# Seven quarter products for piece 10's second layer, and a second engine for some low words

## The chip, the cores and the metric

One core of a Trainium2 chip runs the kernel. The metric is the device time of one execution in microseconds, here the median of three runs. TensorE (PE) multiplies matrices into PSUM; VectorE (DVE), ScalarE (ACT) and GpSimd (POOL) do the element work; GpSimd is given no PSUM operand in this kernel. Each engine takes its instructions in the order in which they were written for it, and a semaphore holds an instruction whose operands or buffers aren't ready.

## The reference

Block-causal attention over q, k, v of 8 batches x 8 heads x 576 x 64, and then a feed-forward network on the 4608 x 512 result:

```
scores = q k^T / sqrt(64);  blocks of 64 columns above the diagonal block are masked
x      = softmax(scores) v                         # (4608, 512), heads side by side
h      = x @ w_in                                  # first layer, 512 -> 2048
g      = h * clip(h + 3, 0, 6) / 6
out    = g @ w_out                                 # second layer, 2048 -> 512
```

Inputs and output are 32-bit floats (the weights arrive as 64-bit words). To reach that accuracy with 16-bit multiplies, the kernel splits each operand into a high word and a low word of 16 bits and adds three products, high x high, high x low and low x high.

## The kernel before

**Tiles and pieces.** The 4608 rows are 13 pieces of up to 384 rows. A piece's first layer makes h in 16 groups f of 128 hidden columns, its second layer adds g of all 16 groups into PSUM banks. Attention runs ahead of the pieces by (batch, head pair) and is done when piece 10 begins. Pieces 10, 11 and 12 (`STR`) run last.

**Plain second layer** (`ffn2_`). For each f and each of three tiles of 128 rows, six matmuls of 512 columns (three word pairs, two halves of 64 stationary columns): 48 groups of six for a piece. Before it, for each f, ACT takes the relu, DVE the product, ACT or DVE the high word and DVE the low word. At the end three banks are copied out.

**Seven quarter products.** Cut into quarters, a product of two matrices of 2 x 2 blocks can be had from seven block products instead of eight, if sums and differences of the blocks are formed first. The first layer of pieces 10 to 12 does this in `h_pair` (seven products for each pair c of groups f; a product is 12 matmuls of 192 columns; ACT and DVE bring it out of PSUM into `hf`, and DVE adds). The weights' sums are made by `w_comb` (one for each of 8 c), the rows' by `x_comb`. The second layer of pieces in `SO` does it in `o_pair`: for a pair c of groups f it runs seven products, each in a part of 256 columns (six matmuls) and a part of 128 columns (six matmuls), into six banks. `g_pair` makes its left operands: relu and product on a pair of groups at once, four sums and differences of 192 columns (`pm`, on DVE or GpSimd), and high and low words of three tiles. `t_comb` makes the combined weights of w_out, `t_homes` says where in SBUF they lie. At the end two scalings and 14 scaled additions bring the seven products into the output rows.

**The order.** The program is first recorded as a list of steps, each with one or more ways (which engine can do it). A table written out in the file, `ORDER`, says for every step in which place and on which engine it is emitted; `SLOTS` says which buffer a tile takes. So the order on each queue, and the choice of engine, are fixed by the tables. PSUM: `h_pair` takes its banks from a pool of two (`ps_h`) and one of three (`ps_s`), but from `ps_h` alone in pieces of `SO` (in the first of them from c = 2 on), since `o_pair` holds the three of `ps_s`.

**Low words of P.** In attention each row block of probabilities is written as high and low words (`phl`) and transposed by a DMA. A row block with an odd number of 64-column blocks ends in a half block of 128 x 64, whose low word is one DVE instruction (line 1156).

Of the kernel before, what the change touches and what calls it, by code (L numbers as in the profile page):

```python
# [56 lines left out]
SO = (11, 12)  # L57
# [26 lines left out]
    "%oBEx1`Qsn7?7C2QU(rmb#{wa(XnjzbcUrzT;r*er^gjO>DzDe<KQeIZ(hbzX;8A2yi_)9{Df@dip-{vi4ny`lSCzA375kcj2L-1"
    "yt!snN?zoU(PL&NrRuKaF3K+m3SOL+6Qv*97CmL<{#h}x#|*RU8>cF+wzMv3Dk~2?6BZJ>blLj$Yj9z%AFrrXTZeUYEmv!%byjWI"
    "xUaXmc4GJQIdwe^FQ(5RpW0Msd*Y<#*YC-v56pd7f8of{M}I!S#ku(S$-zUD{@yS%zZC!F^1P>*&u_ZppS_yDdyn?(%eSjn^{h!q"
    "tf^gVadVvw*0O=Q?e&ijtgTx%Z~tcXJ*oMpQpI-POQE&2PPx_g&Vyrzx4!$)v%lBy0WJjMxbc18Pw(SaI$_Yv+jj;J={NM=Fr2qG"
    "ynT6xD}BbS`?@nLR!+;!Ti_2xFv<qTC2)OL`S=Cs4J4}l&fY7DNduEp@^@V=C`_KWJ2Gm%vGYj!)Yxka7aYsHe)M>GT2WTTNKxgO"
    "(WAx|Z@jd5OE#~nx@6Pkh#_B7_w3F1CXBgoaRh($n(Ys|POe>dVr%qc!M^XaML$lZ9yoY<$DFx`4*&f1`_Hzaw}dxtzFGM8_WBKf"
    "@8sMZzxeLGclRGWd=#+=!^*aQe?4cyB))(vUXnW?udhp=e*Gia_5lN3-Ja~%m^p}-axVEsNou5${DMMj*|3RE-Q_%6bEfJ@R&^+j"  # L90
    "estM0ONR0j!OrTr4W2mI&yz&H@!{C#j~*MNhkH{TMmv7-qFxCIeDQM7V4v8Ac`>j2gI;f{RV)}Y_QVK_;E*t<ku>McqvF;#rZnqU"
    "zJm{It6?TKE#0YU@~zu-Tc%9Cvm?V#tJ_*s_UiK5%q#Pc-(5GZ{N968r_Y>SAO5i7@}tU@KlN1`+8#eS_t$LaQ+07xfAjko-1%MY"
    "nR_idW?6J%ySgt~O_<m-X)@OG!o}X{HYaVLS<g8-W%typv-eo`wd=PJPw=#|rta^5;2_bfWYA!m@1ZzK{ITOF7Lu}aj6R2t40-+L"
    "{m|UJ`~hV}@OgRruEf!`blTVQLhp6X??0R>CNKJ!;5lsjfP%z<=~UVbdj~<%C!Ec<#h=FwO3V29Wv+CCOs;?rS+a7Qi=&e^C3VK~"
    "nX`tkaO*=~Y&*MDwXyEo`0u|M9zT9Asa!Z^s!*h3vcwYhN%yKbt15oYU2s19`^X=^uNk?U7V-3(x7cm|{ow$9HPH|e8P(Y29}pcg"
    "YE1o~(Vg=y1kS&RiTyjGVVT+bHEWxzYxqI6!3Phm+e#+1w6=GUb{{@{hO>0T@)gs1yZX`1{X@F%_N?5v$$3Rzx4^UK>i6_%XbcJt"
    "33UmhY<cp`W$%uA_tpCzJb(D8&2_7`<f&%t^sMY{+u1vtLSKcubEUkOIs@m$>s@c&dJWm11Dn&#c&vWc`SH`|FGbs!{P!9TOJKZu"
    "?RsoW>y4YYZb$SHerQ{=bm*`?#ZjV;uyyTgzbaLcF(Zb{6y7_<@&ZZW`o7U4eSGh|_1oRA|DD%ed-Qia#+B~fu`6}d=mA%*j^Ta$"
    "R9=xbwz8_aW?$U2jP%;1p6+GiCk&iEqjzRqa{S#x6AxcnzH-%@UkQ_D-JhHCdG?$y*RJosG4JN%C%+HOU-0zVYWedQixkR*i&f@p"
    "^70Gl%s(Eiqi~CT^eikIeC%NH*9UHYzh^#+fh+v-)$t=IPO^1+Lt^R0(?epvG0vWQWrlI3((E11{P<}x?9*ps#Q96FFSu{__L(?o"  # L100
    "^A^Hn?87f!gT9Wm@Y{-s9BLV6Yxk|DcEkinr}`BQCC*VRt)d@Qk0X-($Dg`vz3R<({BYlZx2v1i;A{dbr)&uMxpq#~#^ZHALWA~A"
    "B{lvkOW*$|_^(<!ro5tU(^%~7mX14?cUvj^_5%l-es^|t&z(Oq-D;kuXThPvPe#QbOPKjOF81Di!2`3hY14a!BC$j&8-3#G!o;NH"
    "MT?!5I4@mx(xs2*X|F+p*R2m<xZFI0o2pPgw#FSf`fgy~eyM4Tmt+rlcm|iXblI$&Yl}|3e{??c?DE-*m)I>`Ve`T5+=YvmY%s5E"
    "EiPa8yLki4<qaj+roCw=Ua|DQnv&}(;}b@-3TCvm%Y_R9w{0g6!&_~zhCk9$kvQ5e03Sl4^e6A8NrFR(qr69tSvL0S9?}3hBb>=%"
    "zm2o^4Z4-&k+Sz%{5!Qnn5M5bf*LdYeZK)1?BprBg2J(}MaAwuoMcs5$+$@!+fO^LSk=(E!!TjuhiSd%^rho>cI{d@ef63VmE}_t"
    "Dk2lFU#wbmv%2O|ZR5%rO*2<rKC^Jmjqd(E7B_G09yV+C$L8~O0^yuJb1$5|a<x7qbHVD(+=GYiUO&8d?bfX99A55?dGq(Fm3eEA"
    "jEvG~Z{0q+<yg2_)N=36fm0IQ1HBY(>y5;Rk0wohy#M4-BR@(e|N3IG;bru;{Iqn1%Ja$4r^h{FzJ0Iw5j$egv*(+x4WDw~{O8~k"
    "8N=>)W&YZ1=JLCIxc5zp)h#M*Q`ShIvdYn8va7tUhuHVwtRMAY;B8koU%I=4W88ub3v2)U_3^FWTIc5<uq8erw7RCD$;o*m<55fF"
# [1832 lines left out]
```

## Time and profile before

| | |
|---|---|
| three runs | 952.05, 952.43 and 954.31 us, median 952.43 us |
| the profiled execution | 951.95 us, of which the span from first to last instruction is 950.2 us |
| PE busy | 942.8 us (99% of the span) |
| DVE busy | 860.0 us (91%) |
| ACT busy | 722.0 us (76%) |
| POOL busy | 98.3 us (10%) |
| granted TensorE clock | 0.999 of full |

A busy time is the union of an engine's instructions. Matmuls are pipelined and their ends are modelled, so a row's length says less than the distance from its start to the next row's start. Times are counted from the span's start. Almost every instruction stands under line 423, where the recorded steps are emitted, so rows are told apart by the tiles' names: `m` are products of `h_pair`, `hf` what they become, `o` the second layer, `rs`, `gr`, `gs` the operands that `g_pair` makes, `wr`, `wq`, `ws` the tiles of `w_comb`, `tr`, `tw` those of `t_comb` (its results go to `tq`, `tp`, `win`, `vnat`).

### The profile page before, as it was taken

What the parts mean: (1) busy time and instruction counts of PE and PEld (TensorE: products, weight loads), DVE (VectorE), ACT (ScalarE), POOL (GpSimd) and SP (SyncE); (2) the same over time, 40 slices, a digit from 0 to 9 for tenths busy, and PEclk for the clock granted to TensorE, in tenths of its full rate; (3) what the DMA queues carried; (4) which work ended last, traced back from release to release, by engine and by line L of the source; (5) the groups of instructions that cost most, each with busy time, mean ns of one, the idle gap of its engine ahead of it and who ended that gap; (6) DMA issues with size and microseconds to landing.
All of it is one profiled execution on the core that took longest, in us unless ns stands there. A gap on an engine that the chain in (4) does not pass through costs nothing.

```text
span 950.2 us, 34711 instructions
## 1 busy us (share of the span) xinstructions
PE 942.8 (99%) x14108; PEld 686.3 (72%) x14108; DVE 860.0 (91%) x2526; ACT 722.0 (76%) x1791; POOL 98.3 (10%) x283
## 2 busy tenths in 40 slices
PE   9999999999999999999999999999999999999998
PEld 7777777766677766666667666666666667789998
DVE  5988999999999999999999999999899998999987
ACT  6989898888988878888788878778665356676662
POOL 1443101100000000110000010100000102000000
PEclk9999999999999999999999999999999999999999
DMA  7877699989999999999999899986785000000001
GB/s 211 280 246 213 125 178 169 180 166 181 167 189 168 179 188 162 183 189 181 165 201 181 169 165 180 179 162 121 127 128 106 2 2 36 2 35 4 14 26 36
DMA packets 390704, 132.93 MB, mean 140 GB/s; under 512 B 373264, under 2 KB 376592, under 8 KB 390544
## 3 DMA queue, kind: packets, MB, share of 16 engines
q1 hardware_dynamic: 389456, 129.87, 71.7%
q8 instruction: 110, 1.80, 0.8%
q10 hardware_dynamic: 1088, 0.85, 0.3%
q14 instruction: 50, 0.41, 0.1%
HBM read 45.09 MB, written 9.44 MB: 57 GB/s over the span
## 4 chain that ended last, share of the span: by engine, by line
PE 97%; DMA 1%; DVE 1%; ACT 0%; issue 0%; SPq 0%; DVEq 0%
PE o L423 37%; PE h L423 30%; PE m L423 9%; PE s L423 7%; PE pv L423 6%; PE pf L423 1%; PE sf L423 1%; PE pt L423 1%; DMA qkT<-qks 1%; PE pr L423 1%; PE gm L423 0%; DMA qf<-in_q_dram 0%; PE warm L423 0%; PE o_1b L423 0%; PE o_2b L423 0%; PE o_0b L423 0%
## 5 line engine op out<-in xcount | busy, mean ns | idle before, releaser
L423 PE MATMUL o<-wout,g 128*64 128x512 f16 (+2 forms) x2760 | 346.5, 378 | 0.0
L423 PE MATMUL h<-x,win 128*64 128x384 f16 (+2 forms) x3568 | 330.1, 318 | 0.0
L423 PEld LDWEIGHTS <-win 128*64 128x64 f16 (+1 forms) x4432 | 231.7, 110 | 81.3 <-issue 1.7
L423 PEld LDWEIGHTS <-g 128*64 128x64 f16 x2784 | 154.0, 110 | 98.6
L423 DVE SCALAR_TENSOR_TENSOR phl<-p,st,phl 128x64 f16<-128x64 f32 (+4 forms) x364 | 154.9, 447 | 4.2 <-ACT phl L423 2.3
L423 ACT ACTIVATE p<-p,st 128x192 f32<-128x192 f32 (+8 forms) x252 | 139.1, 553 | 22.7 <-DVE st L423 20.7
L423 DVE CUSTOM_DVE_ANT_0 p<-s,none,esc 128x64 f32<-128x64 f32 (+7 forms) x252 | 119.9, 486 | 14.6 <-PE s L423 11.2
L423 ACT ACTIVATE r<-h,eg,sh 128x384 f32<-128x384 f32 (+1 forms) x176 | 101.5, 591 | 40.2 <-PE h L423 33.9
L423 ACT ACTIVATE phl<-p,st 128x512 f16<-128x512 f32 (+5 forms) x173 | 97.2, 582 | 11.2 <-DVE st L423 6.1
L423 PE MATMUL s<-qkT 128*64 128x512 f16 (+7 forms) x1120 | 98.5, 287 | 0.8 <-DMA qkT<-qks 0.8
L423 DVE SCALAR_TENSOR_TENSOR g<-r,g 128x384 f16<-128x384 f32 (+1 forms) x160 | 86.2, 546 | 3.8 <-ACT g L423 3.0
L423 DVE SCALAR_TENSOR_TENSOR r<-r,eg,h 128x384 f32<-128x384 f32 (+1 forms) x144 | 84.2, 586 | 5.8 <-ACT r L423 4.5
L423 ACT ACTIVATE g<-r 128x384 f16<-128x384 f32 (+1 forms) x117 | 58.3, 503 | 18.2 <-PE o L423 11.3
L423 PEld LDWEIGHTS <-qkT 128*64 128x64 f16 x1120 | 53.4, 110 | 25.1 <-DMA qkT<-qks 1.0
L423 PEld LDWEIGHTS <-vhl 128*64 128x64 f16 x1344 | 58.4, 110 | 13.4
L423 PE MATMUL pv<-pT,vhl 128*64 128x192 f16 (+2 forms) x1344 | 67.2, 233 | 0.0
L423 ACT ACTIVATE hf<-m 128x192 f32<-128x192 f32 x90 | 28.5, 327 | 36.9 <-PE m L423 31.9
L423 PEld LDWEIGHTS <-ws 128*64 128x64 f16 x1152 | 52.0, 110 | 4.1
L423 ACT ACTIVATION_READ_ACCUMULATOR p<-p,st 128x1 f32 x252 | 47.7, 189 | 0.0
L423 DVE SCALAR_TENSOR_TENSOR qks<-qk,rs_q,qks 128x576 f16<-128x576 f32 x56 | 46.8, 838 | 0.9 <-ACT qks L423 0.6
L423 PE MATMUL m<-x,ws 128*64 128x192 f16 x864 | 46.8, 246 | 0.0
L423 PE MATMUL m<-x,win 128*64 128x192 f16 x768 | 41.4, 246 | 0.4 <-DVE hf L423 0.4
(229 smaller groups left out, 1414.1 us busy)
## 6 DMA issues: line engine op xcount, KB each, us to landing
vx<-vhl SPq DMA_DIRECT2D x56, 160.0 KB, 3.4
vnat<-in_v_dram SPq DMA_DIRECT2D x63, 128.0 KB, 3.5
qk<-in_k_dram SPq DMA_DIRECT2D x28, 288.0 KB, 4.4
qk<-in_q_dram SPq DMA_DIRECT2D x28, 288.0 KB, 3.9
out_dram<-osb SPq DMA_DIRECT2D x29, 256.0 KB, 2.8
rawo<-in_moe_w_out_dram SPq DMA_DIRECT2D x13, 512.0 KB, 4.9
x<-in_moe_w_in_dram SPq DMA_DIRECT2D x9, 512.0 KB, 5.5
rawi<-in_moe_w_in_dram SPq DMA_DIRECT2D x6, 512.0 KB, 4.8
```

The costliest lines, as they stand in the source:

```text
L423: getattr(eng, method)(*args, **kw)
```

## The change

`SO` becomes (10, 11, 12): piece 10's second layer too is done by `g_pair` and `o_pair`. So `t_comb` is called before piece 10, behind `x_comb` and `w_comb`, and a part of its results gets a home in the tails of the `ws` tiles (`more`). The subtractions of `w_comb`, `x_comb` and `t_comb`, before DVE's alone in the first two, may be GpSimd's too (`plus`, `minus`). `w_comb` makes its sums in two tiles of half the size. A half block's low word may be two instructions of GpSimd: multiply in place, then subtract. In the diff below, `w_comb` and `t_homes` stand in this order; `x_comb`'s four `tensor_sub` become `minus` and `ffn_step`'s call of `t_comb` moves as said, which is left out. The tables are new: the program has 6741 steps instead of 6612, of which GpSimd has 495 instead of 277, DVE 2005 instead of 2190, ACT 1407 instead of 1380.

Read step by step, the new table gives GpSimd 95 of the 140 low words of half blocks, and of the steps recorded from piece 10's `x_comb` on 146 instead of 10 (each an addition or subtraction of two SBUF tiles): 28 `wq`, 30 `tw`, 20 `xt`, 67 `pm`, 1 `xr`. In both tables the steps of DVE and GpSimd can be counted that stand between two places: where PE has done as much work as by 690 us and as by 840 us in the trace of before (each PE step at its length there):

| step | before: DVE, GpSimd | new: DVE, GpSimd |
|---|---|---|
| `wq`, 256 columns | 32, 0 | 4, 28 |
| `tw`, 256 columns | 11, 2 | 2, 30 |
| `xt`, 192 columns | 24, 0 | 3, 20 |
| `pm`, 192 columns | 4, 0 | 0, 36 |
| `tr`, 512 columns | 7, 1 | 16, 0 |
| low words of `t_comb` | 7 | 22 |
| `wr`, of 1024 (new: 512) columns | 6, 2 | 15, 0 |
| `xr`, low words of `x_comb` | 9, 3 and 11 | 11, 1 and 10 |
| plain piece 10: product, low word | 16, 16 | none |
| `g_pair`: product, low words | 2, 1 | 10, 25 |
| attention: low words, softmax | 24, 14 | 11 (5 on GpSimd), 7 |
| high words and copies | 21 | none |

From the later place to the end: `tw` 19 before and none, `tr` 8 and none, low words of `t_comb` 11 and none, `pm` on DVE 58 and 29, on GpSimd 2 and 31, closing additions 28 and 42, high words and copies 7 and 24.

```diff
-SO = (11, 12)
+SO = (10, 11, 12)
...
             if half:
-                nc.vector.scalar_tensor_tensor(
-                    ph[:, last, BLK:], pr[:, nk - BLK:nk], r, ph[:, last, :BLK], op0=ALU.mult, op1=ALU.subtract
-                )
+                ph_, pl, pw_ = ph[:, last, :BLK], ph[:, last, BLK:], pr[:, nk - BLK:nk]
+                nc.add([
+                    ("vector", "scalar_tensor_tensor", (pl, pw_, r, ph_), dict(op0=ALU.mult, op1=ALU.subtract)),
+                    ("gpsimd", [
+                        ("tensor_scalar", (pw_, pw_, r, 1.0), dict(op0=ALU.mult, op1=ALU.mult)),
+                        ("tensor_tensor", (pl, pw_, ph_), dict(op=ALU.subtract)),
+                    ]),
+                ])
...
+    def minus(out, a, b):
+        nc.add([(e, "tensor_tensor", (out, a, b), dict(op=ALU.subtract)) for e in ("vector", "gpsimd")])
...
-        r = attp.tile([P, NDT, NH], F32, tag="qks", bufs=1, name=f"wr{c}")
-        plus(r, win[:, c, :, 0], win[:, c, :, 1])
+        wr = [ffp.tile([P, 2, NH], F32, tag="stage", bufs=NST_B, name=f"wr{c}_{j}") for j in range(2)]
+        for j, r in enumerate(wr):
+            plus(r, win[:, c, 2 * j:2 * j + 2, 0], win[:, c, 2 * j:2 * j + 2, 1])
...
-        nc.vector.tensor_add(o[:, 0], a21, a22)
-        nc.vector.tensor_sub(o[:, 1], o[:, 0], a11)
-        nc.vector.tensor_sub(o[:, 2], a11, a21)
-        nc.vector.tensor_sub(o[:, 3], a12, o[:, 1])
+        plus(o[:, 0], a21, a22)
+        minus(o[:, 1], o[:, 0], a11)
+        minus(o[:, 2], a11, a21)
+        minus(o[:, 3], a12, o[:, 1])
...
-        t = pool.tile([P, 4, 2, 2, P], F16, tag=tag, bufs=bufs, name=f"ws{c}")
+        nu = 2 if tag in ("qkT", "pT2") else 1 if tag == "pT01" else 0
+        t = pool.tile([P, 8 * 2 * P + nu * 2 * DM // 2], F16, tag=tag, bufs=bufs, name=f"ws{c}")
+        more[c] = t[:, 8 * 2 * P:].rearrange("p (i l n) -> p i l n", i=nu, l=2) if nu else None
...
-        rest += [[va[:, i]] for i in range(4)]
+        rest += [[more[3], more[5]], [more[4], va[:, :1]], [more[6], va[:, 1:2]], [more[7], va[:, 2:]]]
```

## Rows read from the trace of the kernel before

**Rows 1.** The page, part 1: busy time, share, instructions.
```profile
PE 942.8 (99%) x14108; PEld 686.3 (72%) x14108; DVE 860.0 (91%) x2526; ACT 722.0 (76%) x1791; POOL 98.3 (10%) x283
```

**Rows 2.** PE's waits, whole span: total us, times, longest us.
```profile
PE s L423 <- DMA qkT<-qks: 0.8, 1, 0.8
...
PE m L423 <- DVE hf L423: 0.4, 1, 0.4
```

**Rows 3.** Windows: length, each engine's busy us (instructions), clock, DMA.
```profile
690.00:740.00 50.00, 50.00 (x664) 32.69 (x660) 46.24 (x123) 29.61 (x68) 3.20 (x9) 1.00 0.62 106
740.00:840.00 100.00, 100.00 (x1552) 72.61 (x1548) 90.76 (x193) 56.03 (x115) 9.16 (x6) 1.00 0.03 10
840.00:945.00 105.00, 104.65 (x2481) 103.06 (x2479) 97.19 (x237) 60.56 (x131) 1.31 (x2) 1.00 0.07 21
```

**Rows 4.** PE's timeline, plain second layer: start us, modelled length us, tile, count.
```profile
815.34 3.40 PE L423 MATMUL o<-wout,g 128*64 128x512 f16 x30
818.58 0.33 PE L423 MATMUL m<-x,win 128*64 128x192 f16 x4
```

**Rows 5.** PE's timeline, seven products, parts of 256 columns.
```profile
923.37 0.52 PE L423 MATMUL o<-win,gs 128*64 128x256 f16 x6
...
924.35 1.18 PE L423 MATMUL m<-x,ws 128*64 128x192 f16 x24
```

**Rows 6.** PE's timeline, seven products, parts of 128 columns.
```profile
943.28 0.53 PE L423 MATMUL o<-win,gs 128*64 128x128 f16 x12
...
943.79 0.86 PE L423 MATMUL o<-vnat,gr 128*64 128x128 f16 x24
```

**Rows 7.** DVE's timeline, as Rows 4, in brackets idle time before.
```profile
744.71 2.37 DVE L423 SCALAR_TENSOR_TENSOR g<-r,g 128x384 f16<-128x384 f32 x1
...
787.23 2.29 DVE L423 TENSOR_TENSOR ws<-wq,ws 128x1024 f16<-128x1024 f32 x1 [0.51 <-ACT ws L423]
...
799.79 0.84 DVE L423 TENSOR_TENSOR tw<-tr,tw 128x256 f32<-128x256 f32 x1
...
912.08 0.89 DVE L423 TENSOR_TENSOR hf<-m,hf 128x192 f32<-128x192 f32 x3 [0.61 <-PE m L423]
```

**Rows 8.** POOL's timeline at the same times.
```profile
744.49 2.18 POOL L423 TENSOR_TENSOR wr<-win 128x1024 f32<-128x1024 f16 x1 [13.52 <-DVE wq L423]
...
786.13 2.31 POOL L423 TENSOR_TENSOR wr<-win 128x1024 f32<-128x1024 f16 x1 [38.28 <-DVE wq L423]
...
798.32 0.73 POOL L423 TENSOR_TENSOR tw<-tr,tr 128x256 f32<-128x256 f32 x1
...
911.99 0.60 POOL L423 TENSOR_TENSOR rs<-rs,hf 128x192 f32<-128x192 f32 x1
```

**Rows 9.** DVE's groups by shape, 690 to 945 us: count | busy us, mean ns.
```profile
L423 DVE SCALAR_TENSOR_TENSOR gs<-rs,gs 128x384 f16<-128x384 f32 x32 | 17.6, 552 | 0.1
L423 DVE SCALAR_TENSOR_TENSOR hf<-rs,eg,hf 128x768 f32<-128x768 f32 x16 | 16.2, 1015 | 0.4 <-ACT rs L423 0.4
L423 DVE SCALAR_TENSOR_TENSOR gr<-hf,gr 128x576 f16<-128x576 f32 x16 | 12.0, 752 | 0.0
...
L423 DVE TENSOR_TENSOR rs<-hf 128x192 f32<-128x192 f32 x31 | 10.5, 353 | 0.2
...
L423 DVE SCALAR_TENSOR_TENSOR r<-r,eg,hf 128x384 f32<-128x384 f32 x16 | 9.7, 614 | 0.5 <-ACT r L423 0.4
...
L423 DVE TENSOR_TENSOR wq<-wr 128x256 f32<-128x256 f32 x16 | 6.6, 419 | 0.1
L423 DVE SCALAR_TENSOR_TENSOR osb<-o,so,osb 128x256 f32<-128x256 f32 x14 | 6.5, 478 | 0.3
```

**Rows 10.** DVE's groups by shape, 0 to 740 us: the half blocks' low words.
```profile
L423 DVE SCALAR_TENSOR_TENSOR phl<-p,st,phl 128x64 f16<-128x64 f32 x140 | 39.2, 284 | 2.4 <-ACT phl L423 1.4
```

**Rows 11.** POOL's groups by shape, whole span: the nearest to the new pair.
```profile
L423 POOL TENSOR_SCALAR qks<-qks 128x576 f16<-128x576 f16 x26 | 20.9, 802 | 71.7 <-DVE qks L423 43.0 <-ACT qks L423 22.9 <-DVE pp L423 3.4
L423 POOL MEMSET p<- 128x64 f32 x112 | 16.2, 160 | 213.6 <-DVE phl L423 171.3 <-ACT phl L423 11.0 <-ACT qa L423 10.5
```

More of the change, by code (lines that the diff above doesn't have):

```diff
@@ L84 @@
[L84 to L108, printed above, removed]
@@ new lines @@
+    "rsf^}yH_>rnNBO;nVPnG#>`m<=$m#`=iRuzkFodQo44uv*Ke~sa{JCLs{OIWYYrV>JA2N}zgXP2U*ESIojLp9=Y-$q?%uoq&iE+h"
+    ";l#ssw&%&8E_|M3^5sh7)y<c;Y<>2JYI-sA>-%dNm+VIRK7aAjZ^_bSuY6wrAdmtA@kGy{tU+@>SX%j0y{zpW96#ENB~mBG37bdW"
+    "Lx;--CnYlFK|`D!ToT-A7*|#X-OMAt`P9kNrA1E$44nKpB%9Bjm-$p2oMJ95lZ+^zkfU9Z)e<^Ur!Sr)C=rS{Y@XYw(T5{j>&B$!"
+    "M-3Z0Zf0_t>Pp_Cg2LdC#p$`x>hT>hQ&#Su6&rU<GrO^Qs_bf8`;wN5%CIxxp<zpxt?#_HW9P2x$E&I%EW*2bmPaW1x@$IU+}B@Q"
+    "Ke6}uoQ7#lFQ(5Rp4!x4ed46z*YC-v56peoc;U#=M}Iz@J$L@%<0l6XP5OJo$oNvim&@~>ntXoKoAB(_{M~z$Uthjmy=vN;#H70V"
@@ new lines @@
+    "wWc@MSz*kY7~5X|_`uw{W%KrL=HHWBf6ComS$j#8w)QEvI^KD(ZLk)1KY9-G8adbzhc7K3@P4|JOW6ePnYZr@9X4?Iy%CmhMRYFj"
+    "a;D9gbzgO6#mc_C`~?AEf?hEsK9S?M%GW<ots#(YclKXNN*<DuTCnSCVNuGw-BHo=wcSTDrp8@cxZqgU^`plt(~GmKMhmLPjU6*y"
+    "zwy%MEjiqp+LBF|b;G`<?b)08jURjA;wawgHQOKboLsx^#MYR{Zu`E^7W_DscHrRY9dqU$I{fq3??2my-{Rl6`DWqU+v_*{y_0*h"
+    "eDU3T@9sZ%_(-?NgqdUe{(A0&Njx`>a7o_a`~i+m0|!O9+6E4Bc6qX2VPq#<%D&_mEvgfX3JQxXBqJt1Wl6c##tio(*|lMow4=+O"
+    "nbGB+a5m=8t+4o^{+<NljSt5@fArWGGt!4-H<s-0b)0(QORVhuAk%;smp{CG<?B5(VAIyXplz?O#!-StEg0Pt(ww?-^SJe)N_BDl"
@@ new lines @@
+    "m@Lfr_*K-^Yc#Ft8QWVjv+W&jO`bAUl{N47+I4r@2RBqy!sY$&R8@7`snd@iJle74NloOdj>gVXO!(6-(=%6|{rPKTY|?EC%e}K_"
+    "TK~-Hy|ZRV=(U$EcE3J3;L@B46W3c=+nDt+CQY8QVd^#W8N1$KuUPJ(lz4jWJ8FJm@BWJi4ll%cA3QYB!jeSJ@y#7H6rY!W?6}vF"
+    "x5EmG?2F&MAASP<Y!)ppS@ModDP20)E&l6}4<9jRWd!24AIp5c&t0C7sQ>Jc^u;lG#EKQRcGS`HN2Z+o`Ah69k$&3Xm+2z2mn+py"
+    "G|$wUMRd+LChPl;@}C*MbSiB?U|N|~1D6-+?xFeZnqI{hu39Zv{5xt%G#0;r5EJ`nW3~4%_&%7uX3D~;aY1u}ZAMizHm$FmiyJ;-"
+    "%-Y@a#$7yL8$uj=fL&ML+|qi%_~4<Sb@08_9Tqx&`KGq^&Yo$9Pj4RCwW2rtZ^Y6qMvAT5S2i}Caq3&vzhR@u`AOl^XD>}QZRTv*"
@@ new lines @@
+    "wqwuTy^i<J-UpVQ72_W~9PsF|%ek!|2hyHr@5{-}+vY$I3y&mm8P>{(Vnu#|lm3cp$8^<xjpK{XSFd?*cJ40e-t+d|RhIVs2j;cw"
+    "H@3GG7Im@R_&V_?wdC{OFLGfNH`;yO0FhL1^H$7l*{;~QQ9H(r9(!lklC^iP_AK@BZSP1MIB31!veK{P%gQ~*rDsl<=s#_G-`h!*"
+    "Rrjjn6E_U58In<3_i^8+-ui~O$tkZte!Bnbcj}D(YcpppUpfEi>^baJtJln(cm2lQH)b~z{ye5Jo;-cVeE#CIblq9m%dBHx<nH;0"
+    "3Wg>vSXel@Xwk4+w+}D&@cjJu>o*tr@%;x(jgA!SFC9E_^2=8fuUPMA&tJHbDYh3cnY>b|jlaMAac;!v2g67GWPSUt(T*y+V2YVw"
+    "cmCDG*N@D7txI%q)dAEqQ4=Rk9=XD1rRA!+`qH#?49?yMAH6!p&w}XitHVDqsN9V3XNtMS)QVH#P0ef8hSqF6jtvWLZ4ZfPQz$oB"
@@ L234 @@
+    "H?h!G_g^?tMTbbc^}nwLtTYcx-Xgg5O@F!8@@{7jl&?OPt1dh^j9Y}LV9ddz)c3k?D!S<M#twG=uO9;=)niW$f!BA<Xa8jRwj-}Z"
+    ")E^}a39<"
 )
@@ L1299 @@
     sw = {}
+    more = {}
     homes = []
@@ L1453, in t_comb @@
         o = attp.tile([P, 4, NM], F32, tag="phl1", bufs=1, name=f"tw{c}")
-        def minus(out, a, b):
-            nc.add([(e, "tensor_tensor", (out, a, b), dict(op=ALU.subtract)) for e in ("vector", "gpsimd")])
         minus(o[:, 0], b12, b11)
@@ L1746, in ffn_step @@
             pc, f = divmod(done1, NFT)
-            if pc == SO[0] and f == 0:
-                was = nc.key, nc.cls, nc.grp
-                nc.cls = "a"
-                homes.extend(t_homes())
-                for c in range(NCH):
-                    nc.grp = 3200 + c
-                    t_comb(c)
-                nc.key, nc.cls, nc.grp = was
             if pc in STR and f == 0:
@@ L1765, in ffn_step @@
                         w_comb(c)
+                nc.key, nc.cls, nc.grp = was
+            if pc == SO[0] and f == 0:
+                was = nc.key, nc.cls, nc.grp
+                nc.cls = "a"
+                homes.extend(t_homes())
+                for c in range(NCH):
+                    nc.grp = 3200 + c
+                    t_comb(c)
                 nc.key, nc.cls, nc.grp = was
```

275 lines of the change are left out of this document (142 added, 133 removed).

## The prediction

> **What bounds the kernel now.** I read the page's first part, then what PE waited for, then the windows of the last stages, then timelines. PE is busy 99% of the span [rows 1], and three waits of 1 us or less are nearly all that the trace finds [rows 2]. Since the ends of matmuls are modelled, "busy" alone proves little; but from start to start PE runs at one rate wherever I look: six matmuls of 512 columns take (818.58 - 815.34) / 5 = 0.648 us [rows 4]. So time is what PE's instructions add up to, and an edit can win only by making them fewer, or lose by letting PE run dry. The engine nearest to that is DVE: 46.24 + 90.76 = 137.0 us busy of the 150 from 690 to 840 us, and 97.19 of the 105 behind them [rows 3]. POOL is nearly idle there (3.20, 9.16, 1.31 us).
>
> **The change, part by part.**
>
> *PE.* Plain, piece 10's second layer is 48 groups of six matmuls: 48 x 0.648 = 31.1 us [rows 4]. With seven products it is 8 x 7 = 56 parts of 256 columns at (924.35 - 923.37) / 3 = 0.327 us [rows 5] and 56 of 128 columns at (943.79 - 943.28) / 3 = 0.170 us [rows 6]: 56 x 0.497 = 27.8 us. PE's work falls by 3.3 us. The first layer keeps its products.
>
> The Trainium skill ("TensorE: Matmul & The Clock Gate", section "Back-to-back issue gap") speaks against this: it gives a sustained 81 ns for a matmul of 128 columns and 131 ns for one of 512, so that small parts would pay for their weight loads; by an estimate from it the plain form would be 288 x 131 = 37.7 us and the seven products, with some 98 ns at 256 columns, 336 x 81 + 336 x 98 = 60 us. The rows decide otherwise for weights of 64 columns: 0.170 / 6 = 28 ns and 0.648 / 6 = 108 ns.
>
> *DVE and POOL, from 690 to 840 us of PE's work.* This is where the new table packs `w_comb`, all of `t_comb` (half of it lay behind 840 us) and piece 10's `g_pair`. Instructions overlap at their ends: three adds of 192 columns take 0.89 us, the last 0.35, so one takes 0.27 and not 0.353 [rows 7, 9]; I take 0.08 off each mean. From the counts of steps that front of this text lists:
> - leave DVE: 37 adds of 256 columns at 0.34 and 25 of 192 at 0.27, 19.3 us; 16 products at 0.53 and 16 low words at 0.47 of the plain form, 16.0; 13 low words of attention, 7 softmax steps and 21 high words or copies, 41 at some 0.38 (an estimate between 0.27 and 0.47), 15.6;
> - come: 8 products of 768 columns at 0.93, 7.4; 24 low words of `g_pair` at 0.54 (0.67 and twice 0.47), 13; 9 `tr` of 512 columns and 15 low words of `t_comb`, which I price between 0.34 and 0.67 at 0.54, 13; the smaller `wr` and the rest, 2.5.
>
> That is -51 + 36 = -15 us [rows 9]. The 137.0 us hold also waits for POOL, which I take out next: 4.5 us. Own work: 137.0 - 4.5 - 15 = 117.5 us.
>
> *What POOL's steps cost DVE.* This decides. At 744.71 DVE began a low word of two SBUF inputs that takes 0.55 us alone; it ran 2.37 us, to 747.08, because POOL was adding from 744.49 to 746.67. The same happened at 787.23 (2.29 us for 1.22) and at 799.79 (0.84 for 0.42); five such instructions, from the first of these to the last, waited 4.5 us together [rows 7, 8]. DVE's adds from PSUM at 912.08 ran at their rate beside POOL's step of 911.99. So a step of POOL on two SBUF tiles and an instruction of DVE on two SBUF tiles exclude each other. DVE went on at 747.08 - 0.55 = 746.53, 0.14 us before POOL's record ends; with some 0.1 us at its start (my estimate) a step of POOL holds the port for its length less 0.24 us. The ten such steps of before, 11.0 us undisturbed, held it 8.6 us and cost DVE 4.5: 52%.
>
> In the new table's stretch there are 115 steps: 58 of 256 columns at 0.73 - 0.24 = 0.49, 56 of 192 at 0.60 - 0.24 = 0.36 [rows 8], one longer at 0.7: 49 us held. At 52%, DVE waits 26 us: 117.5 + 26 = 143 of 150 us. Bounds: nothing lands on DVE (117.5), or all of it (167, PE 17 us late). I take 52%, the only share that the trace has, and with it DVE stays just under PE; before it was at 137. PE ran into DVE once, for 0.4 us [rows 2]; at 95% instead of 91% I expect another such wait or two, 0.5 us.
>
> *Behind 840 us* DVE loses 19 `tw`, 8 `tr`, 11 low words and 29 `pm` (6.5 + 4.8 + 5.5 + 7.8 us at the prices above) and gets 14 closing additions and 17 copies or high words (some 0.34 and 0.27: 9.3 us), and 31 steps of POOL hold 11 us: 97.2 - 15.3 + 6 = 88 of 102 us. That is looser than before.
>
> *Low words of half blocks.* 95 of the 140 leave DVE, 95 x 0.20 = 19 us over attention [rows 10]. POOL's pair isn't in the trace: its first step lies between a fill of 128x64 (0.160) and a multiply of 128x576 (0.802) [rows 11], nearest the fill, 0.25; its second between 0.160 and the 0.60 of 192 columns [rows 8], 0.3. Pair: 0.32 to 1.4, I take 0.55, of which some 0.3 held; at 52% DVE gets 15 us back as waits. So DVE gains from 19 down to -26 us (0.5 us held in full for all), probably 4, spread over 640 us; PE's one wait for attention is 0.8 us for a DMA [rows 2], and while that cover lasts the price is nothing either way. Without it a row block's transpose starts half a microsecond later.
>
> *At nothing:* five more output DMAs on SP's queue, when input has ended (DMA share 0.03 to 0.07 [rows 3]); one more closing of 16 steps, as between pieces 11 and 12, and `h_pair` from two PSUM banks instead of five, as in these pieces: with both PE idled 0.35 us in 105 [rows 3]. ACT has 44 us free of the 100 from 740 us on [rows 3].
>
> **Sum.** The profiled execution took 951.95 us (950.2 of span, 1.75 around it): 951.95 - 3.3 + 0.5 = 949.2. The median of the three runs lies 0.48 us higher, so 949.7 us, 0.29% under it. A run-to-run change of this kernel under 0.3% (2.9 us) can't be told from none; the forecast lies on that edge.
>
> **The rivals.**
> - *The port overflows (slower).* 115 steps in 150 us lie much denser than ten in 255. DVE's PSUM work, behind which POOL can go free, is then used up, and the share that lands on DVE rises. The point: 117.5 + 49 s = 150 at s = 0.66. From there PE waits for `hf` adds and operands that stand behind the blocked instruction on DVE's queue. At s = 0.8 DVE needs 157 us, 7 late: 952.4 - 3.3 + 7 = 956; at 1.0, 966. For it: the blocks of rows 7 are whole, not shared. Against: 52% was measured with DVE just as full.
> - *Half the gain goes in small waits (no change).* DVE's and POOL's chains feed each other in `g_pair` (product, four sums on POOL, words), and one block of 0.4 us at a tight product stalls PE: 24 pairs c in pieces 10 to 12, 0.1 us each, 2.4 us: 951.6. For it: one wait of this kind exists. Against: in the 40 pair steps of before's last three pieces (24 of `h_pair`, 16 of `o_pair`) there is one only.
> - *All of the gain and old waits go (faster).* 3.3 + 0.8 + 0.4 = 4.5 us: 948.0. For it: DVE is looser behind 840 us. Against: the DMA's wait has nothing to do with the change.
> - *Weight loads bound the small parts (slower).* PE's loads are busy 103.06 of 105 us behind 840 [rows 3]. Were piece 10's 672 loads not hidden as there, at a fifth of their 0.11 us shown each, 15 us: 964. Rows 5 and 6 show them hidden; 1 in 100.
>
> **How the numbers follow.** The forecast has 0.43, with its own range 948.9 to 950.6; it falls about half under 0.3%. Small waits 0.14, all of the gain 0.12, the port 0.30, weight loads 0.01. Faster by over 0.3%: 0.12 + 0.22 = 0.34. Within 0.3%: 0.21 + 0.14 = 0.35. Slower: 0.31. The range that holds 8 of 10 goes from 948.5 to 957: some 0.06 below, and above it the port at shares over 0.8 with 0.13.
>
> **What would show it.** PE's groups at 0.327 and 0.170 us in piece 10, and 27.8 us in all (the gain). PE's waits for DVE: two or three, under 1 us together; ten or more on `hf`, `gs` or `gr` between 740 and 840 us mean that the port has overflowed. DVE busy about 143 us from 690 to 840 with `wq`, `ws`, `gs`, `tr` longer in the mean than now; were their means unchanged, POOL's steps cost DVE nothing. POOL's steps of 192 columns at 0.6 to 0.8 us. The prediction is wrong if DVE's blocked time comes near to POOL's 49 us, or if PE idles for a product of GpSimd itself.

## The result, and the profile after

The changed kernel took 960.98 us (median of four runs, 959.07 to 962.1) against 952.24 for the kernel before beside it: a ratio of 1.0091, 95% interval 1.0061 to 1.012. It is slower by 8.7 us, outside the range of 948.5 to 957; the forecast was 949.7. The profiled execution took 960.49 us, with a span of 958.7. The later comparisons each have runs of the kernel before of their own (medians 950.6 to 951.4), so kernels are compared below by their ratios; 0.1% is about 1 us. Two slow executions, 978.64 us of the kernel before and 3459.96 us of the kernel without `rs`, are left out of the ratios.

Part 1 of the page, and the first line of part 4, the chain that ended last; below them part 4's line of the kernel before:

```profile
PE 943.4 (98%) x14492; PEld 709.3 (74%) x14492; DVE 850.1 (89%) x2341; ACT 731.8 (76%) x1817; POOL 283.4 (30%) x596
...
PE 80%; DVE 9%; POOL 3%; ACT 3%; DMA 3%; issue 2%; SPq 0%; DVEq 0%; ACTq 0%; POOLq 0%
```
```profile
PE 97%; DMA 1%; DVE 1%; ACT 0%; issue 0%; SPq 0%; DVEq 0%
```

DVE is less busy than before [rows 1], yet 9% of the chain now runs through it; before, the page had PE 97% and DVE 1%. What PE waited for (as [rows 2]):

```profile
PE m L428 <- DVE hf L428: 1.6, 3, 0.8
PE o L428 <- DVE gr L428: 1.3, 2, 1.0
PE o L428 <- DVE gs L428: 1.2, 2, 0.7
PE m L428 <- ACT hf L428: 1.2, 2, 0.8
...
PE pv L428 <- DVE st L428: 0.9, 1, 0.9
PE pv L428 <- DMA pT<-phl: 0.9, 2, 0.6
```

Windows (as [rows 3]), and the 160 us from 690 to 850 in one, the last line being the kernel before:

```profile
690.00:740.00 50.00, 49.42 (x662) 33.11 (x660) 44.32 (x88) 32.86 (x71) 25.88 (x41) 1.00 0.46 92
740.00:840.00 100.00, 94.49 (x1718) 81.90 (x1715) 91.08 (x135) 56.74 (x118) 72.40 (x81) 1.00 0.03 10
840.00:945.00 105.00, 104.13 (x2500) 103.03 (x2499) 92.11 (x198) 55.27 (x121) 31.13 (x43) 1.00 0.07 18
...
690.00:850.00 160.00, 153.51 (x2601) 124.34 (x2599) 144.59 (x237) 96.45 (x203) 106.92 (x132) 1.00 0.16 35
```
```profile
690.00:850.00 160.00, 160.00 (x2418) 114.17 (x2414) 146.18 (x337) 93.59 (x201) 12.36 (x15) 1.00 0.23 44
```

PE loses 5.5 us between 740 and 840, at a clock of 1.00. As ends of matmuls are modelled, I measured standstill from start to start as well: wherever the next instruction starts over 0.1 us later than that kind does on average in the kernel before. Summed, in us (it comes out above what the windows leave idle: 9.5 us against 160 - 153.51 = 6.5 in the late stretch, since a modelled end reaches into a gap):

| kernel | before 690 | 690 to 850 | behind | span less these |
|---|---|---|---|---|
| before | 2.7 | 0.0 | 0.6 | 946.8 |
| after | 5.1 | 9.5 | 0.9 | 943.2 |

So PE's own work fell by 3.6 us, and 12.2 us of standstill came, 9.5 of them in the stretch from 690 to 850.

DVE's groups in that stretch, by shape. Before, `gs`, `hf` and `gr` were at 552, 1015 and 752 ns [rows 9]:

```profile
L428 DVE TENSOR_TENSOR tr<-wout 128x512 f32<-128x512 f16 x16 | 14.6, 912 | 2.0 <-POOL wq L428 1.9
L428 DVE SCALAR_TENSOR_TENSOR hf<-rs,eg,hf 128x768 f32<-128x768 f32 x10 | 12.2, 1219 | 2.6 <-ACT rs L428 2.6
L428 DVE SCALAR_TENSOR_TENSOR gs<-rs,gs 128x384 f16<-128x384 f32 x16 | 12.1, 768 | 0.0
L428 DVE SCALAR_TENSOR_TENSOR gr<-hf,gr 128x576 f16<-128x576 f32 x9 | 10.5, 1167 | 0.0
L428 DVE TENSOR_TENSOR win<-tw,win 128x256 f16<-128x256 f32 x8 | 5.3, 668 | 1.1 <-ACT win L428 1.1
```

POOL's groups there, and its pairs over the whole span:

```profile
L428 POOL TENSOR_TENSOR rs<-hf 128x192 f32<-128x192 f32 x18 | 14.4, 810 | 8.1 <-DVE hf L428 8.1
L428 POOL TENSOR_TENSOR tw<-tr,tw 128x256 f32<-128x256 f32 x16 | 14.2, 887 | 0.9
L428 POOL TENSOR_TENSOR wq<-wr,wr 128x256 f32<-128x256 f32 x7 | 7.5, 1069 | 9.8 <-DVE wr L428 5.8 <-DVE tq L428 3.1 <-DVE vnat L428 0.4
...
L428 POOL TENSOR_SCALAR p<-p,st 128x64 f32<-128x64 f32 x95 | 46.4, 488 | 207.3 <-ACT phl L428 123.9 <-DVE phl L428 83.3
L428 POOL TENSOR_TENSOR phl<-p,phl 128x64 f16<-128x64 f32 x95 | 38.9, 409 | 7.9
```

And seven microseconds of it (start, length; left out are the weight loads, ACT's lines, most of PE's, two of POOL's and one of DVE's):

```profile
821.73 1.48 DVE L428 SCALAR_TENSOR_TENSOR hf<-rs,eg,hf 128x768 f32<-128x768 f32 x1
822.35 2.04 POOL L428 TENSOR_TENSOR rs<-hf 128x192 f32<-128x192 f32 x2
...
823.13 0.81 DVE L428 TENSOR_TENSOR vnat<-tw,vnat 128x256 f16<-128x256 f32 x1
...
823.86 1.08 DVE L428 TENSOR_TENSOR ws<-tw,ws 128x512 f16<-128x512 f32 x1
824.09 0.49 PE L428 MATMUL o<-vnat,gr 128*64 128x256 f16 x6
824.42 0.49 PE L428 MATMUL o<-wout,gr 128*64 128x256 f16 x6
824.47 0.92 POOL L428 TENSOR_TENSOR rs<-rs,hf 128x192 f32<-128x192 f32 x1
...
824.87 0.81 DVE L428 TENSOR_TENSOR win<-tw,win 128x256 f16<-128x256 f32 x1
825.60 1.54 DVE L428 SCALAR_TENSOR_TENSOR gs<-rs,gs 128x384 f16<-128x384 f32 x2
825.75 0.98 POOL L428 TENSOR_TENSOR wq<-wr,wr 128x256 f32<-128x256 f32 x1 [0.36 <-DVE win L428]
826.20 0.47 PE L428 MATMUL o<-ws,gs 128*64 128x256 f16 x8 [0.74 <-DVE gs L428]
...
827.07 1.28 DVE L428 SCALAR_TENSOR_TENSOR gr<-hf,gr 128x576 f16<-128x576 f32 x1
...
828.40 0.25 PE L428 MATMUL o<-wout,gr 128*64 128x128 f16 x2 [0.97 <-DVE gr L428]
```

DVE starts one step as the last ends, each longer than its shape is alone (`gr` 1.28 for 0.75), and PE's two long waits here are for DVE's low words `gs` and `gr`. The parts of 256 columns start 0.33 us apart, as forecast.

Ten microseconds earlier a wait of another kind stands:

```profile
811.97 0.52 ACT L428 ACTIVATE gs<-rs 128x384 f16<-128x384 f32 x1 [1.84 <-POOL rs L428]
...
813.45 1.48 DVE L428 SCALAR_TENSOR_TENSOR hf<-rs,eg,hf 128x768 f32<-128x768 f32 x1 [1.96 <-ACT rs L428]
...
814.21 0.69 PE L428 MATMUL m<-vnat,ws 128*64 128x192 f16 x12 [0.82 <-ACT hf L428]
```

ACT waits 1.84 us for one of GpSimd's sums, what follows on ACT's queue comes late, and behind it DVE is idle for 1.96 us and PE for 0.82. So a part of the standstill is the chain through GpSimd and not a full DVE.

### The profile page after: what moved, and what is told of

Its sections match the earlier page's. It is cut to its first block, busy times and chain, and to the rows that moved or that the text cites. A ratio compares the mean times of both kernels' runs of the same rounds, so it can differ in the third digit from the quotient of the medians.

```text
span 958.7 us, 35735 instructions
## 1 busy us (share of the span) xinstructions
PE 943.4 (98%) x14492; PEld 709.3 (74%) x14492; DVE 850.1 (89%) x2341; ACT 731.8 (76%) x1817; POOL 283.4 (30%) x596
## 4 chain that ended last, share of the span: by engine, by line
PE 80%; DVE 9%; POOL 3%; ACT 3%; DMA 3%; issue 2%; SPq 0%; DVEq 0%; ACTq 0%; POOLq 0%
PE o L428 29%; PE h L428 26%; PE s L428 7%; PE m L428 6%; PE pv L428 5%; PE sf L428 1%; PE pt L428 1%; POOL wq L428 1%; DVE ws L428 1%; PE pf L428 1%; DVE hf L428 1%; DVE gs L428 1%; DMA pT<-phl 1%; DVE tr L428 1%; ACT p L428 1%
## 5 line engine op out<-in xcount | busy, mean ns | idle before, releaser
L428 PE MATMUL o<-wout,g 128*64 128x512 f16 (+2 forms) x2472 | 312.8, 378 | 0.0
L428 PEld LDWEIGHTS <-g 128*64 128x64 f16 x2496 | 144.2, 110 | 83.2
L428 ACT ACTIVATE p<-p,st 128x512 f32<-128x512 f32 (+8 forms) x252 | 138.9, 552 | 13.3 <-DVE st L428 12.3
L428 DVE SCALAR_TENSOR_TENSOR phl<-p,st,phl 128x512 f16<-128x512 f32 (+4 forms) x269 | 133.0, 509 | 2.5 <-ACT phl L428 1.4
L428 ACT ACTIVATE phl<-p,st 128x256 f16<-128x256 f32 (+5 forms) x183 | 102.3, 583 | 16.3 <-DVE st L428 6.2
L428 POOL TENSOR_SCALAR p<-p,st 128x64 f32<-128x64 f32 x95 | 46.4, 488 | 207.3 <-ACT phl L428 123.9
L428 DVE SCALAR_TENSOR_TENSOR g<-r,g 128x384 f16<-128x384 f32 (+1 forms) x144 | 78.4, 549 | 2.9 <-ACT g L428 2.1
L428 ACT ACTIVATE g<-r 128x384 f16<-128x384 f32 (+1 forms) x103 | 50.5, 497 | 11.7 <-DVE r L428 6.4
L428 PEld LDWEIGHTS <-gs 128*64 128x64 f16 x1152 | 53.6, 110 | 2.0 <-DVE gs L428 1.9
L428 POOL TENSOR_SCALAR st<-st 128x3 f32<-128x3 f32 x36 | 9.1, 253 | 150.8 <-ACT p L428 141.6
```

The source lines that it names most:

```text
L428: getattr(eng, method)(*args, **kw)
```

## The experiments

### Does it matter which engine makes the late sums?

Three kernels take late sums from GpSimd to VectorE, where the table would have them on GpSimd. The edits (the first part stands in all three and sends a step to VectorE where the table's engine is no longer among its ways; the second is for `rs`, the third for `wq`, `tw`, `xt`, `xr`; the third kernel has all of them):

```diff
             o.eng = self.NAMES[hi // 32]
+            if o.eng not in o.ways:
+                o.eng = "vector"
...
-            nc.add([(e, "tensor_tensor", (out, a, b), dict(op=op)) for e in ("vector", "gpsimd")])
+            nc.add([("vector", "tensor_tensor", (out, a, b), dict(op=op))])
...
-        nc.add([(e, "tensor_tensor", (out, a, b), dict(op=ALU.add)) for e in ("vector", "gpsimd")])
+        nc.add([("vector", "tensor_tensor", (out, a, b), dict(op=ALU.add))])
```

(and the same for the subtraction.)

> The changed kernel with the 67 sums of quarters of h (rs) that were on GpSimd now on VectorE, all else as it is. 36 of them lie between 690 and 850 us. Theory A (VectorE's load decides, and GpSimd's two-input steps lengthen what VectorE does beside them, 31.6 us for 95 steps there, 0.33 us each): VectorE gains 36 x 0.35 = 12.7 us of own work and loses 36 x 0.33 = 12 us of lengthening, so nothing moves: 960 to 961.5 us. Rival B (the latency of the chain through GpSimd decides: three sums of 0.81 us in a row against 0.35 us on VectorE, with TensorE waiting behind them): the stalls between 690 and 850 halve, 956.5 us.

> The changed kernel with the 79 sums of weight blocks and x blocks (wq, tw, xt, xr) that were on GpSimd now on VectorE; the sums of h stay on GpSimd. 59 of them lie between 690 and 850 us. Theory A (VectorE's load): 59 x (0.40 - 0.33) = 4 us more for VectorE in that stretch, 961 to 965 us. Rival B (latency through GpSimd): these sums take 0.72 to 1.07 us there and 0.35 to 0.42 on VectorE, so what TensorE waits for comes earlier: 958 us.

> The changed kernel with all 146 late sums on VectorE, none on GpSimd; the low words of P stay as changed. Theory A (VectorE's load): 44.5 us of own work more and 31.6 us of lengthening less between 690 and 850 us, so that VectorE has 157 us to do in 160: the stalls grow from 9.5 us to 14 or more, 965 us. Rival B (latency through GpSimd decides, VectorE has room): the stalls of that stretch fall to 2 or 3 us, 953 to 955 us.

Measured: 1.0104 (1.0089 to 1.0119), 1.0105 (1.009 to 1.0121) and 1.0116 (1.0101 to 1.0131) of the kernel before; 960.75, 960.9 and 961.68 us. None differs from the changed kernel by more than the intervals hold; between 690 and 850 us PE stands still 10.0, 10.3 and 10.0 us (9.5). Latency through GpSimd (rival B, 953 to 958 us) is out as the main cause; and the loss does not need the port, because with all sums on VectorE there is nothing for it to exclude and the time is no shorter. The groups of the third kernel show that the same load is now made of other steps:

```profile
L430 DVE TENSOR_TENSOR tr<-wout 128x512 f32<-128x512 f16 x16 | 10.9, 683 | 0.0
...
L430 DVE SCALAR_TENSOR_TENSOR gs<-rs,gs 128x384 f16<-128x384 f32 x16 | 8.7, 549 | 0.6 <-ACT gs L430 0.6
L430 DVE SCALAR_TENSOR_TENSOR gr<-hf,gr 128x576 f16<-128x576 f32 x9 | 6.8, 750 | 0.4 <-ACT gr L430 0.4
...
690.00:850.00 160.00, 152.45 (x2581) 127.78 (x2577) 150.59 (x347) 95.14 (x201) 5.97 (x18) 1.00 0.15 35
```

DVE's steps have their own lengths again, and it makes 110 more of them. Theory A's own figure for this kernel, 965 us with 14 us or more of standstill, was missed as well: 961.68 and 10.0. And 1.8 us of the standstill in the second and third kernel have a cause of their own, which the changed kernel does not have:

```profile
DVE wq L430 <- DMA pT<-phl: 2.5, 1, 2.5
PE s L430 <- DVE st L430: 1.8, 1, 1.8
```

The first `wq` now waits on VectorE's queue until a transfer of P has left the buffer that they share, and PE waits behind it. So the times agree in part by chance.

### What are the sums worth?

Here the sums are left out. In the first kernel GpSimd writes zeros instead, for all 146; three others do so for one name each; one shortens the `rs` of the kernel with all sums on VectorE.

```diff
+                if o.eng == "gpsimd" and method == "tensor_tensor" and len(o.ways[o.eng]) == 1:
+                    eng.memset(args[0], 0.0)
+                    continue
                 getattr(eng, method)(*args, **kw)
```

(for one name: `args[0].tensor.name[:2] in ("wq",)`, `("tw",)` or `("rs",)` instead of the length.)

> The changed kernel with each of the 146 late sums on GpSimd replaced by a GpSimd write of zeros of the same size (the sums are left out, so the second layers are computed from zeros). It reads nothing, and is shorter (0.15 us for 64 columns in this trace, an estimate of 0.3 to 0.4 us for 192 to 256). Theory A (what VectorE has to do between 690 and 850 us is the bound: the sums cost it about as much as lengthening of its own steps, 31.6 us, as they would cost it itself, 42 us): without them VectorE has 131 us to do in 160, the 9.5 us of stalls there fall to 1.5 or less, 952 to 954 us. Rival B (the new order of the steps on TensorE and ScalarE, or the due times of the transfers): 958 us or more.

> The changed kernel with only the 28 sums wq (weight blocks of the first layers) that GpSimd makes replaced by GpSimd writes of zeros of the same size, so these sums are left out; all other sums stay. All 28 lie between 690 and 850 us, 27.6 us of GpSimd's time there, out of 101.5 for its two-input sums; the kernel before makes them in that stretch as well, on VectorE. Theory A (the whole load of the stretch is the bound, and a sum costs the same whichever it is): 27% of the 12 us that leaving out all the sums gave, 957.7 us. Rival B (only what the change brought forward is late, the wq are in time): 960 to 961 us.

> The changed kernel with only the 30 sums tw (weight blocks of the second layers, which the change wants one piece earlier) that GpSimd makes replaced by GpSimd writes of zeros, so these sums are left out. All 30 lie between 690 and 850 us, 28.5 us of GpSimd's time. Theory A (load, whichever sum): 28% of 12 us, 957.6 us. Rival B (the second layer of piece 10 waits for these steps, due one piece earlier, in the order in which they stand): most of the 12 us, 952 us.

> The changed kernel with only the 67 sums rs (quarters of h) that GpSimd makes replaced by GpSimd writes of zeros, so these sums are left out; 36 of them lie between 690 and 850 us (29.6 us of GpSimd's time), 31 behind (21 us). Theory A (load): 29% of 12 us, and little behind 850 us, where TensorE hardly waits: 957.3 us. Rival B (the chain through them is what TensorE waits for): 953 us.

```diff
-            nc.add([(e, "tensor_tensor", (out, a, b), dict(op=op)) for e in ("vector", "gpsimd")])
+            nc.add([("vector", "tensor_tensor", (out[:, :1], a[:, :1], b[:, :1]), dict(op=op))])
```

> The kernel with all late sums on VectorE (e4_all_sums_dve, 961.7 us), and the sums of quarters of h reduced to their first column (the others are left out): 36 x 0.28 = 10 us less for VectorE between 690 and 850 us, nothing on GpSimd there in either. A dose of VectorE work alone. Theory A: VectorE's load is the bound in that stretch, whose stalls (10 us) fall to 2 or 3: 953 to 955 us. Rival B (order of the steps): 960 us or more.

| kernel | ratio to before (95%) | median us | PE stands still, 690 to 850 |
|---|---|---|---|
| no sums | 0.9975 (0.9962 to 0.9987) | 948.95 | 0.3 |
| no `wq` | 1.0044 (1.0027 to 1.006) | 956.08 | 4.4 |
| no `tw` | 1.0045 (1.0028 to 1.0061) | 956.62 | 3.9 |
| no `rs` | 1.0028 (1.0016 to 1.004) | 954.57 | 3.0 |
| `rs` of one column, rest on VectorE | 1.0067 (1.0044 to 1.009) | 957.27 | 6.7 |

Without the sums the late standstill is gone and PE's gain shows: 948.95 us, below even the 952 to 954 of theory A. The new order by itself is thus not what costs. By the ratios all of the sums are worth 11 us, and any one name 4.4 to 6, the old `wq` as much as the `tw` that the change wants earlier: the loss does not hang on one late step. Each gave more than its expected share (3.2 to 3.5), and together they give nearly 15, more than all at once: what is taken off first counts most. `rs` came nearer to the figure for the chain through it (953) than to that for load (957.3), with an interval that touches the others'; whether it costs more than its load stays open. The shortened `rs` gave 4.7 us of the 7 to 9 expected.

The windows of the kernel without sums, the forecast's own stretch in three parts:

```profile
690.00:740.00 50.00, 50.00 (x674) 32.42 (x672) 41.71 (x92) 33.47 (x72) 12.25 (x45) 1.00 0.45 91
740.00:790.00 50.00, 50.00 (x736) 35.56 (x734) 38.69 (x75) 29.76 (x63) 9.26 (x38) 1.00 0.03 10
790.00:840.00 50.00, 49.98 (x1194) 49.48 (x1190) 37.27 (x73) 31.71 (x68) 11.95 (x51) 1.00 0.04 12
```

DVE: 41.71 + 38.69 + 37.27 = 117.7 us where the prediction put its own work at 117.5. Beside GpSimd's writes of zeros, which read nothing, its steps kept their lengths: 2.4 us over the tenth percentile of their shapes in these 150 us, as with no late step on GpSimd (2.2). The Trainium skill ("SBUF — State Buffer", section "SBUF: two separate sides") has the port that the two engines share locked for a whole instruction, against VectorE's steps with two SBUF inputs only where GpSimd's step reads SBUF; the trace agrees.

### Was the kernel before already at the edge?

If the load is the cause, the kernel before, whose DVE was busy 146.18 of these 160 us while PE was idle for none of them, must pay for any load that is added to it. Two kernels make sums `wq` of the kernel before twice; a third puts them on GpSimd.

```diff
+DOUBLE = ("wq1", "wq3", "wq5", "wq7")
...
                 getattr(eng, method)(*args, **kw)
+                if o.eng == "vector" and args[0].tensor.name[:3] in DOUBLE:
+                    getattr(eng, method)(*args, **kw)
```

(all eight names in the second.) And the third, so for all four sums, with the table's VectorE turned to GpSimd for them:

```diff
-        nc.vector.tensor_add(o[:, 0], a21, a22)
+        nc.add([("gpsimd", "tensor_tensor", (o[:, 0], a21, a22), dict(op=ALU.add))])
```

> The kernel before with 16 of its 32 sums wq (those of every second chunk) made twice on VectorE, which changes nothing but VectorE's load: 16 x 0.42 = 6.7 us more between 690 and 850 us, where VectorE was busy 146 of 160 us and TensorE never waited. Theory A (at 91% VectorE was already as full as this stretch allows, so that what is added comes out at the end): about 40% of the dose as in the runs that took sums away, 954 us. Rival B (TensorE waits only when VectorE has no time left, at 160 of 160): 951 to 952 us.

> As the run with half of them, with all 32 sums wq made twice on VectorE: 13.4 us more between 690 and 850 us. Theory A: 957 us. Rival B: with 159.6 of 160 us asked of VectorE, 952 to 953 us.

> The kernel before with its 32 sums wq on GpSimd instead of VectorE, all else unchanged: VectorE has 13.4 us less of its own between 690 and 850 us, and is lengthened by GpSimd's steps (0.33 us each in the changed kernel, 10.6 us). Theory A (the sums cost VectorE nearly the same on either engine): 950.5 to 953 us. Rival B (the chain through GpSimd, 0.9 us a sum, makes the first layers' weights late by itself): 955 us or more. Rival C (it relieves VectorE): 949 us.

Measured: 1.0036 (1.0023 to 1.005), 1.0102 (1.0087 to 1.0117), 1.0013 (1.0003 to 1.0022); 953.75, 959.77 and 951.62 us. Theory A held for the half dose and for the third kernel; the whole dose cost 9.2 us, more than the 6 that it gave. The stretch from 690 to 850 us in the three, in this order:

```profile
690.00:850.00 160.00, 157.69 (x2333) 115.70 (x2331) 149.78 (x348) 91.05 (x196) 11.94 (x16) 1.00 0.23 45
```
```profile
690.00:850.00 160.00, 153.29 (x2218) 113.24 (x2216) 150.25 (x347) 85.45 (x184) 11.93 (x16) 0.99 0.22 41
```
```profile
690.00:850.00 160.00, 160.00 (x2424) 114.35 (x2422) 141.67 (x305) 93.57 (x202) 39.31 (x47) 1.00 0.22 43
```

DVE (third of the busy times) gets to some 150 of these 160 us, 94%, and no further, however much is asked: that is also where it stood with all late sums (150.59 above). That is no limit of the engine, for in that kernel it was busy 59.56 of the 60 us from 720 to 780, and PE still 59.84:

```profile
720.00:780.00 60.00, 59.84 (x826) 47.84 (x824) 59.56 (x132) 33.67 (x65) 0.00 (x0) 1.00 0.07 19
```

The rest is time in which DVE itself waited, for ACT, PE or a transfer. From 146 to 150 PE already stands still 2.8 us; of the second dose 4.9 us more of 6.7 come out as standstill (7.7 in all). In time it cost 6.0 us, and here the clock has a share:

```profile
750.00:760.00 10.00, 7.80 (x82) 5.21 (x78) 9.35 (x22) 2.59 (x4) 0.99 (x1) 0.85 0.01 2
760.00:770.00 10.00, 10.00 (x142) 8.19 (x140) 9.79 (x20) 3.36 (x6) 0.00 (x0) 0.98 0.01 2
```

PE had stood idle for 2.20 us before 757.03, and for a while behind that the granted clock was at its lower level, 1.2 GHz: 1.5 + 0.2 = 1.7 us of full clock are missing in these two windows, which is the most that this can have cost, and all five executions of this kernel have a mean of 0.997 or 0.998.

Busy time alone does not decide, though. Without `tw` the changed kernel's DVE was busy less than the kernel before's, and PE still stood still 3.9 us; the third kernel here had about as much (141.67) and PE was never idle:

```profile
690.00:850.00 160.00, 158.13 (x2717) 130.81 (x2715) 140.91 (x251) 99.95 (x213) 88.95 (x136) 1.00 0.16 36
```

How early the steps are due in each order counts too; that was not tested by itself. The third kernel also shows the price of GpSimd's help: 32 x 0.42 = 13.4 us of sums left DVE, and its busy time fell by 146.18 - 141.67 = 4.5.

### The low words of P

Four kernels: the changed one with them on VectorE (the GpSimd way taken out of the list at line 1164), with all 140 as pairs, and with a write of zeros in place of each pair; and the kernel before with the 95 pairs. A fifth leaves out the pair's first step.

```diff
-                    ("gpsimd", [
-                        ("tensor_scalar", (pw_, pw_, r, 1.0), dict(op0=ALU.mult, op1=ALU.mult)),
-                        ("tensor_tensor", (pl, pw_, ph_), dict(op=ALU.subtract)),
-                    ]),
```

> The changed kernel with the low words of P's odd half blocks on VectorE again, as before (95 steps of one instruction); the late sums stay on GpSimd. Of the 12.2 us that TensorE stands still more than in the kernel before, 2.4 us lie before 690 us of the profile and 9.5 us between 690 and 850. Theory A (the pairs cause the early part, since 214 VectorE steps beside them are 16 us longer than their shapes are otherwise): 958.5 us, the early stalls back to 2.7 us. Rival B (the pairs cost nothing, the early stalls come from the new order of the steps): 961 us, early stalls stay at 5 us. Rival C (the pairs do relieve VectorE, which has 95 x 0.28 = 27 us more to do without them): 963 us or more.

```diff
+            if o.eng == "vector" and len(o.ways.get("gpsimd", ())) == 2:
+                o.eng = "gpsimd"
```

(in the kernel before with the change's two ways for the step, and with `and o.n not in KEPT`, the 45 steps that the change leaves on VectorE.)

> The changed kernel with all 140 low words of the odd half blocks as pairs of GpSimd instead of 95. Theory A (each pair relieves VectorE, and 95 of them are worth 6.1 us): 45 more give up to 2.9 us, but only 2.4 us of stalls are left before 690 us: 958 to 960 us. Rival B (the 45 were left on VectorE because what waits for them is near; 0.9 us instead of 0.28 us): 962 us or more.

> The kernel before with only the pairs: the same 95 low words of P's odd half blocks as two steps of GpSimd, its own order and all else unchanged. In the changed kernel taking the pairs back cost 6.1 us. Theory A (the pairs relieve VectorE, but TensorE stands still for only 3.3 us in the kernel before, 1.4 of these at the start): 950 to 951.5 us, no change. Rival B (the pairs gain wherever they are): 946 to 948 us. Rival C (a pair is 0.9 us instead of 0.28 until the transfer of P can start, and the order has no room for that): 954 us or more.

```diff
-                        ("tensor_scalar", (pw_, pw_, r, 1.0), dict(op0=ALU.mult, op1=ALU.mult)),
-                        ("tensor_tensor", (pl, pw_, ph_), dict(op=ALU.subtract)),
+                        ("memset", (pl, 0.0), {}),
```

> The changed kernel with each of the 95 pairs of GpSimd replaced by one GpSimd write of zeros of 64 columns (0.15 us; the low words of these half blocks are left out). Theory A (the pairs cause the early stalls): early stalls fall from 5.1 us to 3 or less, 958.5 us. Rival B (the order causes them): they stay at 5 us, 960 to 961 us.

> The changed kernel with the pairs of GpSimd cut to their second step: the scaling of P by 1/sum before the subtraction is left out, so that a low word takes 0.41 us of GpSimd instead of 0.49 + 0.41. Theory A (the 2.4 us of stalls before 690 us that the change adds come from the pairs, which hold back the transfer of P and lengthen VectorE's steps): the early stalls fall from 5.1 to 3.5 us or less, 959 us. Rival B (they come from the order): early stalls stay at 5 us, 961 us.

Measured: on VectorE 1.017 (1.0152 to 1.0187), 967.1 us; all 140 as pairs 1.0128 (1.0106 to 1.0149), 963.17; in the kernel before 1.0059 (1.0039 to 1.0079), 956.72; zeros 1.009 (1.0076 to 1.0105), 959.05; the second step alone 1.0087 (1.0072 to 1.0103), 960.23. The first lies beyond even rival C's 963 us, the second is as rival B and the third as rival C had it. Moving these words costs 3.5 to 7.5 us in every direction, so what a pair is worth cannot be read from a swap. That each order suits only the engines that it was made for is the likely reason, and not shown. In the kernel before, the longest new wait is for P's transfer, behind the longer pairs, and after its 2.0 us the granted clock fell in the profiled execution (0.83 from 250 to 260 us, 1.7 us of full clock missing). Other executions as long show a mean clock of 1.0, so beyond the wait it stays open what the 5.6 us are made of:

```profile
PE pv L431 <- DMA pT<-phl: 2.7, 2, 2.0
```
```profile
250.00:260.00 10.00, 8.03 (x104) 5.81 (x102) 6.36 (x21) 5.02 (x13) 1.32 (x6) 0.83 0.86 127
```

(The 16 us by which the first expectation has VectorE's steps longer beside the pairs, and the 31.6 us of the late stretch, counted waits inside DVE's semaphore instructions too; without these the second is about 30, and the first between 5 and 11, by what is taken as a step's own length.) Making the pairs all but free changed nothing (1.009 against 1.0091), so they are not shown to cost the changed kernel anything. Its 2.4 us of early standstill stay open: kernels that share its first 690 us (those of the two sections on the late sums) had 3.1 to 6.3 us of it in their profiled executions, so a single profile cannot carry so small a difference.

## Why the prediction was wrong, point by point

- **PE's work, -3.3 us:** right. 3.6 us by the standstill table, and the kernel without sums is 2.4 us faster than before by its ratio.
- **DVE's own work, 117.5 us of 150:** right, as the kernel without sums shows.
- **What POOL's steps cost DVE, 26 us:** right. DVE's steps between 690 and 840 were 27.9 us longer than the tenth percentile of their shapes, against 2.2 with no late sum on GpSimd: 25.7 us. The parts it was made of were not: GpSimd's sums were longer (104 there took 94.2 us, 0.91 each, not 0.60 to 0.73), and so the share that landed on DVE was smaller than the 52%: by the prediction's own 0.24 us less for each they held 94.2 - 104 x 0.24 = 69 us, and 25.7 of that is 37%. That the product came out is luck.
- **The step that failed: 143 of 150 us "stays just under PE", 0.5 us of waits.** The sum came out, 117.7 + 25.7 = 143.4; reading it against 150 as if all the rest were room was wrong. The kernel before, at 91% [rows 3], was at the edge for its order: 3.2 us are lost to the first 6.7 us added to it, about what the change was expected to add (143 - 137.0). The changed kernel had 144.59 us busy to 850 and 9.5 us of standstill, more than that dose makes. What the new order and the chain through GpSimd have in the rest stays open. That PE had waited for DVE's words only once, for 0.4 us [rows 2], was taken for slack, and the mean over 150 us hides where a step is due: from 821.73 to 828.35 DVE has no gap at all, and PE waits there.
- **The rivals.** That DVE would overflow had 0.30 and the right place and sign; but its condition, a share over 0.66, did not come about, and its price at the measured share was nothing. "Half the gain goes in small waits" had the kind of wait (words of `g_pair`, tight products, and sums of GpSimd that hold up ACT and then DVE) at a quarter of the size.
- **The signs.** `tr` (912 ns instead of 686), `gs` and GpSimd's sums became longer, as they should. DVE's busy time from 690 to 840 us by the clock was 44.32 + 91.08 = 135.4 and not 143, since PE was late by then and the work of the stretch reached to about 850 (144.59). PE's waits for `hf`, `gr` and `gs` were seven and 4.1 us in all: neither the two or three under 1 us nor the ten that were to mean an overflow.
- **Behind 840 us, looser:** right as to DVE, 92.11 us busy instead of 97.19; standstill behind 850 grew by 0.3 us.
- **The pair, 0.55 us:** 0.488 + 0.409 = 0.90; the first step is not near the fill (0.160) but halfway to the longer multiply [rows 11]. That they cost nothing is not contradicted and not shown.

No version here that makes all its sums beats the kernel before: what seven products save on PE, 3.6 us, is bought with more vector work than these orders had room for.
